# Layer two of an attention and feed-forward kernel: the output product of the third pair of token blocks by seven block products

## The chip, the core and the metric

The kernel is one program on one core of a Trainium2 chip. Its time is the device time of one execution in microseconds (us); of a kernel that ran several times the median is given. TensorE is called PE below, VectorE DVE, ScalarE ACT, GpSimd POOL, and SyncE, which issues the DMAs, SP.

## What is computed

Causal attention with a decay, and then two feed-forward layers on 2304 tokens of 512 values. The change lies in the second layer, `_moe2_ref`:

```python
def reference(**kwargs):
    ...
    attn_out = _attn_ref(**attn_kwargs)
    x = attn_out.transpose(0, 2, 1, 3).reshape(B * S, H * D)   # 2304 x 512
    x = _moe_ref(x=x, **moe_kwargs)
    return _moe2_ref(x=x, **moe2_kwargs)

def _moe2_ref(x, w_in, w_out, alpha):        # w_in 512 x 2048, w_out 2048 x 512
    h = x @ w_in
    g = np.maximum(h, 0.0) + alpha * np.minimum(h, 0.0)
    return (g @ w_out).astype(np.float32)
```

## The kernel before

**Tiling.** The 2304 tokens are three pairs of token blocks, a block being 384 tokens (`NB`); a pair p has its results in the tile `R[p]`. The 2048 middle features are eight groups g of 256, and a group is two feature blocks of 128. One step of the program is a *set* (layer, g, p). In layer two the sets with p = 0 and 1 come first, for all groups; then the sets with p = 2, in the group order 6, 7, 0, 1, 2, 3, 4, 5, close the program.

**A set's input product** is `x @ w_in` on its pair and group, a product of 2 by 2 blocks. It is already made with seven block products instead of eight (`product`, named 1, 5, 6, 3, 7, 2, 4 in their order), each of six matmuls of 384 columns: two slices of the contraction by three terms. A number is kept as a rounded high part and a low rest, and the terms are high by high, high by low and low by high. PSUM sums are completed by ACT copies (`keep`) and DVE additions (`add`). `activate` then makes g of one token block n and feature block i: `first` (ACT, Relu), `second` (DVE), `third` (ACT casts the high part, POOL subtracts it for the low part).

**A set's output product** is `g @ w_out`. It is made as six pieces (`piece`), one for every 128 tokens, each of six matmuls of 512 columns: two feature blocks by three terms. Here g is the stationary operand. DVE adds each piece from its PSUM bank (three of them, `ps_o`) to `R[p]` (`flush`); in the first group of a pair ACT copies instead, and in the last group a DMA writes the rows out.

**Order.** All engines work in the order in which the program was written. A set's seven products are interleaved with the pieces of the set before it, as a string says: `SEQ[1] = "1q5q6q3q7q2q4"`, where q is a piece and every character is one step. `later(d, ...)` puts work behind the step d characters on, `aside(d, ...)` the same, after `later`'s. After the last set six pieces run alone (the *drain*).

**Side work.** During the sets with p = 0 the float64 weights of the next group are converted: tables as `CONV_EVEN` name operations (`ho0`, `lo0` and so on) and the steps at which they run. Converted weights are kept in DRAM, and the sets with p = 2 load them again (`load_w`: 1792 KB of `wi` and 1024 KB of `wo`).

Of the kernel before, what the change touches and what calls it, by code (L numbers as in the profile page):

```python
# [8 lines left out]
F32 = mybir.dt.float32  # L9
# [12 lines left out]
def decay_attention_ffn2_kernel(ctx, tc, qk, v, f, wi1, wo1, wi2, wo2, alpha, out):  # L22
# [59 lines left out]
    wi_d = [[dram.tile([128, 2, 7 * KH * 128], F32, name=f"wid{ff}{g}") for g in range(NG)] for ff in range(2)]  # L82
    wo_d = [[dram.tile([128, 2, FT * DM], F32, name=f"wod{ff}{g}") for g in range(NG)] for ff in range(2)]

    f_d = [dram.tile([128, 4, KH * 256], F32, name=f"fd{g}") for g in range(NC)]
# [36 lines left out]
    def conv_ops(ff, g, cache=False, held=(), tags="abdbc"):  # L122
# [46 lines left out]
        def combine(name):  # L169
            d, a, b, op = SUM[name]  # L170
            nc.gpsimd.tensor_tensor(out=blk(*d), in0=blk(*a), in1=blk(*b), op=op)

        PART = {"a": (0, 2, 0, 0), "b": (2, 4, 1, 0), "c": (4, 6, "S", 0), "d": (6, 7, 1, 0), "o0": 0, "o1": 1}

# [34 lines left out]
        for name in SUM:  # L209
            ops[name] = lambda name=name: combine(name)  # L210
        for name in PART:
            ops["h" + name] = lambda name=name: high(name)
            ops["l" + name] = lambda name=name: low(name)
# [66 lines left out]
    def attention():  # L280
        with ExitStack() as ax:
# [399 lines left out]
    for ff in range(2):  # L681
        sets += [(ff, g, p) for g in gorder[ff][0] for p in range(NPR - 1)]
        if ff == 0:
            sets[1:3] = [(0, 1, 0), (0, 0, 1)]
        sets += [(ff, g, NPR - 1) for g in gorder[ff][1]]
    slot_of = {(0, 0): 0, (0, 1): 1, (0, 2): 0, (1, 0): 1, (1, 1): 0, (1, 2): 1}

    now, at, behind = [0], {}, {}

    def later(d, fn):  # L690
        at.setdefault(now[0] + d, []).append(fn)
# [4 lines left out]
    def activate(s, gt, i, n, h, d):  # L696
        ff, g, p = s
        if n not in gt:
            gt[n] = {}
        hold = {}  # L700

        def first():
            t = P["tp"].tile([128, NB], F32, tag="t", name="t")
# [16 lines left out]
        def third():  # L720
            gt[n][i] = P["gp"].tile([128, 2, NB], F32R, tag=f"g{n}", name=f"g{n}", bufs=3 - n)
            nc.scalar.copy(out=gt[n][i][:, 0], in_=hold["g"])  # L722
            nc.gpsimd.tensor_sub(out=gt[n][i][:, 1], in0=hold["g"], in1=gt[n][i][:, 0].bitcast(F32))  # L723

        later(d, first)
        later(d + 1, second)
        later(d + 1, third)

# [37 lines left out]
    def piece(s, gt, n, c):  # L766
# [35 lines left out]
        later(0, flush)  # L802

    def side_work(s):

        ff, g, p = s

        def conversion(ops, text, keep, scale=1, shift=0, first=0, last=10 ** 6):
            for name, t in table(text, first, last):
                if keep or name[0] != "w":  # L810
                    aside(t * scale + shift, ops[name])
# [14 lines left out]
        if p == 0 and (1 if ff else 2) <= g + 1 < NG and not (ff == 0 and g < 2):  # L826
            ops, keep = conv_ops(ff, g + 1), g + 1 < NG - 2
            cached = ff == 1 and g + 1 < NC
            for text in ((CONV_TURN if cached else CONV_EVEN,) if ff else (CONV_A, CONV_B)):
                conversion(ops, text, keep, 1, 3 if ff and not cached else 5)  # L830
        if p == NPR - 1:
# [21 lines left out]
    def run():  # L853
        prev = None
        for q, s in enumerate(sets + [None]):
            pieces = []
            if prev is not None:
                ps, pgt = prev
                pieces = [lambda n=n, c=c: piece(ps, pgt, n, c)
                          for n in (1, 0) for c in range(KD if ps[0] == 0 else NB // 128)]  # L860
            c, gt = {}, {}
            if s is None:
                seq = "q" * len(pieces)
            else:
                seq = FIRST[q] if q < len(FIRST) else SEQ[ps[0]]
            if s is not None and q != 1:
# [83 lines left out]
```

## Time and profile before

| what | value |
|---|---|
| median of three runs | 960.58 us (960.13 to 962.03) |
| the profiled execution | 962.06 us, its span 960.3 us, granted TensorE clock 0.998 |
| busy in the span | PE 950.0 us, DVE 695.9, POOL 593.6, ACT 535.2 |
| layer two, p = 2, before the drain | eight sets, 822.1 to 948.23 us, 15.77 us each |
| drain | 948.23 to 957.35 us, then the last DMA |

The busy time of PE counts matmuls that overlap, so that 99% does not mean that no matmul waited. The times that matter here are distances between starts.

### The profile page before, as it was taken

How to read it: one execution, taken by the hardware profiler on the slowest of the kernel's cores; microseconds unless marked ns; L12 is line 12 of the kernel's file. 1: busy time of each engine (PE TensorE's matmuls, PEld its weight loads, DVE VectorE, ACT ScalarE, POOL GpSimd, SP SyncE). 2: the span in 40 equal slices, each digit the busy share in tenths (PEclk: the TensorE clock that was granted, in tenths of full speed). 3: DMA queues.
4: the chain of work that ended last, by engine and by line, in shares of the span. 5: the costliest groups of instructions: out<-in, count | busy, mean ns of one | idle time of the engine just before them, and what ended most of it. 6: DMA issues, size and time to landing. Idle time of an engine off the chain costs nothing.

```text
span 960.3 us, 15782 instructions
## 1 busy us (share of the span) xinstructions
PE 950.0 (99%) x5525; PEld 860.1 (90%) x5525; DVE 695.9 (72%) x1227; ACT 535.2 (56%) x1316; POOL 593.6 (62%) x586
## 2 busy tenths in 40 slices
PE   8999999999999999999999999999999999999998
PEld 5777777798999999999999999989899898999897
DVE  7899998858687877786788565267789777535454
ACT  5888887856654555554644365645444545443231
POOL 7678998666666466585765299546655659423131
PEclk9999999999999999999999999999999999999999
DMA  6666777301444244111677623414534410344441
GB/s 217 220 192 205 221 243 212 110 23 44 160 181 160 104 187 187 66 44 34 223 294 292 255 77 125 161 56 165 186 116 159 174 58 34 113 184 164 198 165 66
DMA packets 36195, 145.79 MB, mean 152 GB/s; under 512 B 4860, under 2 KB 4860, under 8 KB 33012
## 3 DMA queue, kind: packets, MB, share of 16 engines
q1 hardware_dynamic: 36112, 144.79, 42.6%
q8 instruction: 43, 0.70, 0.3%
q14 instruction: 36, 0.29, 0.1%
q10 hardware_dynamic: 4, 0.00, 0.0%
HBM read 97.21 MB, written 43.42 MB: 146 GB/s over the span
## 4 chain that ended last, share of the span: by engine, by line
PE 92%; DVE 4%; POOL 1%; issue 1%; ACT 1%; DMA 1%; ACTq 0%; DVEq 0%; SPq 0%; POOLq 0%
PE o L780 21%; PE hA L740 20%; PE o L778 20%; PE hC L740 10%; PE hB L740 5%; PE tp L420 4%; PE pv L478 4%; PE sc L389 2%; PE sc L390 2%; PE sc L401 1%; PE sc L403 1%; PE sc L391 1%; PE tr L458 1%; POOL xl L250 1%; PE pv L510 0%
## 5 line engine op out<-in xcount | busy, mean ns | idle before, releaser
L723 POOL TENSOR_TENSOR g<-t,g 128x384 fp32r<-128x384 f32 x192 | 205.6, 1072 | 284.0 <-ACT g L722 267.5
L778 PE MATMUL o<-g,wo 128*128 128x384 f32 x1152 | 230.8, 339 | 1.2 <-POOL g L723 1.1
L740 PE MATMUL hA<-xh,wi 128*128 128x384 f32 x768 | 224.2, 337 | 0.6 <-ACT p L372 0.3
L780 PE MATMUL o<-wo,g 128*128 128x512 f32 x864 | 223.2, 394 | 0.0
L778 PEld LDWEIGHTS o<-g,wo 128*128 128x128 f32 x1152 | 204.1, 188 | 2.4 <-POOL g L723 2.0
L722 ACT CAST g<-t 128x384 fp32r<-128x384 f32 x192 | 98.7, 514 | 176.6 <-DVE t L717 91.9
L780 PEld LDWEIGHTS o<-wo,g 128*128 128x128 f32 x864 | 160.6, 188 | 25.7
L798 DVE TENSOR_TENSOR r<-o,r 128x512 f32<-128x512 f32 x126 | 86.7, 688 | 86.1 <-PE o L780 85.7
L740 PEld LDWEIGHTS hA<-xh,wi 128*128 128x128 f32 x768 | 141.5, 188 | 4.1 <-DVE hD L754 0.6
L740 PE MATMUL hA<-xl,wi 128*128 128x384 f32 x384 | 129.6, 337 | 0.0
L787 DVE SCALAR_TENSOR_TENSOR r<-o,r 128x384 f32<-128x384 f32 x168 | 92.3, 553 | 46.8 <-PE o L778 45.9
L740 PE MATMUL hC<-xh,wi 128*128 128x384 f32 x384 | 114.1, 338 | 0.0
L372 ACT ACTIVATE p<-sc,nm 128x128 f32<-128x128 f32 (+2 forms) x144 | 80.3, 561 | 20.2 <-DVE nm L365 16.6
L365 DVE TENSOR_REDUCE nm<-sc 128x1 f32<-128x128 f32 (+2 forms) x144 | 71.5, 507 | 13.2 <-PE sc L391 8.2
L740 PEld LDWEIGHTS hA<-xl,wi 128*128 128x128 f32 x384 | 72.1, 188 | 3.2
L740 PEld LDWEIGHTS hC<-xh,wi 128*128 128x128 f32 x384 | 70.9, 188 | 2.1 <-issue 0.2
L250 POOL TENSOR_TENSOR xl<-r,xh 128x384 fp32r<-128x384 f32 x59 | 68.5, 1173 | 2.1 <-ACT xh L245 1.6
L420 PE MATMUL tp<-ident,p 128*128 128x128 f32 x384 | 66.7, 276 | 0.3 <-ACT pt L435 0.3
L745 ACT COPY s<-hA 128x384 f32<-128x384 f32 x96 | 45.8, 477 | 36.1 <-PE hA L740 35.8
L740 PE MATMUL hC<-xl,wi 128*128 128x384 f32 x192 | 64.8, 337 | 0.0
L740 PE MATMUL hB<-xh,wi 128*128 128x384 f32 x192 | 57.1, 338 | 0.0
L754 DVE TENSOR_TENSOR hC<-hC,s 128x384 f32<-128x384 f32 x48 | 27.1, 564 | 40.7 <-PE hC L740 38.9
(150 smaller groups left out, 1744.5 us busy)
## 6 DMA issues: line engine op xcount, KB each, us to landing
wid<-wi SPq DMA_DIRECT2D x24, 896.0 KB
wi<-wid SPq DMA_DIRECT2D x12, 1792.0 KB
rqk<-in_qk SPq DMA_DIRECT2D x32, 608.0 KB
raw<-in_wi SPq DMA_DIRECT2D x32, 512.0 KB
raw<-in_wo SPq DMA_DIRECT2D x32, 512.0 KB
wod<-wo SPq DMA_DIRECT2D x24, 512.0 KB
wo<-wod SPq DMA_DIRECT2D x12, 1024.0 KB
vt<-in_v SPq DMA_DIRECT2D x16, 320.0 KB
```

Of the source, the lines that this page charges most:

```text
L250: e.tensor_sub(out=XS[k][1][:, b, c], in0=x, in1=XS[k][0][:, b, c].bitcast(F32))
L365: last = waits("V", nc.vector.tensor_reduce(out=nm, in_=src, axis=AX.X if n == 1 else AX.XY, op=ALU.max, negate=True), last)
L372: last = waits("A", nc.scalar.activation(out=o, in_=src, func=AF.Exp, bias=nm, scale=1.0, accum_out=dst), last)
L420: nc.tensor.transpose(tp[:, j, :], pt[:, 128 * j:128 * j + 128], ident)
L722: nc.scalar.copy(out=gt[n][i][:, 0], in_=hold["g"])
L723: nc.gpsimd.tensor_sub(out=gt[n][i][:, 1], in0=hold["g"], in1=gt[n][i][:, 0].bitcast(F32))
L740: nc.tensor.matmul(out=h, lhsT=a, rhs=b[:, x, kc], start=new and kc + e == 0, stop=kc == KH - 1 and e == 2, skip_group_check=not new)
L745: nc.scalar.copy(out=c[k], in_=h)
L778: nc.tensor.matmul(out=o[:, 0:NB], lhsT=a[:, cs], rhs=b, start=st, stop=sp)
L780: nc.tensor.matmul(out=o, lhsT=b[:, cs], rhs=a, start=st, stop=sp)
L787: later(0, lambda: nc.vector.scalar_tensor_tensor(out=acc, in0=o[:, 0:NB], scalar=1.0 / 6.0, in1=acc, op0=ALU.mult, op1=ALU.add))
L798: nc.vector.tensor_add(out=acc, in0=o, in1=acc)
```

## The change

For the first seven of the eight groups of pair 2 in layer two (the list `seven`) the output product too is made with seven block products of the 2 by 2 blocks of g (two token blocks by two feature blocks) and of `w_out` (two feature blocks by two halves of 256 columns). The eighth group stays as it was. A block product is three chunks of 128 tokens by three terms: nine matmuls of 256 columns, so 63 of 256 columns for a set in place of 36 of 512. They stand in eleven pieces (`PLAN7`): "4" is two chunks of product 4, "45" the third chunks of 4 and 5 in one bank, "7-" the third chunk of 7 alone. The products are summed over the seven groups in places of their own (`kept`: the four quarters of `R[2]`, two raw tiles, one `wb` tile) and combined in the last of the sets (`sum7`). Sums of blocks of g are made by POOL (`sums`), and each of the seven left operands has its own ACT cast and POOL subtraction. Differences of weight blocks are made in the conversion (`t1` to `t4` on POOL; `v1` to `v4` on DVE for groups 7 and 0), written to DRAM (`wt_d`), loaded as 512 KB for a set and split by two casts on ACT and two subtractions on DVE (`weights7`).

```diff
+    SEQ7 = "1q5qq6qq3qq7qq2q4q"
+    PLAN7 = ("4", "5", "45", "1", "6", "16", "7", "7-", "2", "3", "23")
+    LAST7 = "v1 54 v3 54 v2 55 u0 55 v4 55 u1 56"
+    WT7 = {5: 0, 7: 1, 4: 2, 6: 3}
...
+        def differ(name):
+            b11, b12, b21, b22 = (f32(2 + t)[:, k] for t in range(2) for k in range(2))
+            d, a, b = {"1": (b11, b12, b11), "3": (b12, b22, b12), "2": (b22, b22, b11), "4": (b21, b22, b21)}[name[1]]
+            (nc.vector if name[0] == "v" else nc.gpsimd).tensor_sub(out=d, in0=a, in1=b)
...
-    CONV_EVEN = "... ho1 28 lo1 29 wi0 40 wi1 43 wo0 46 wo1 48"
+    CONV_EVEN = "... ho1 28 lo1 29 t1 29 t3 29 t2 30 u0 30 t4 30 u1 31 wi0 40 wi1 43 wo0 46 wo1 48"
...
+        def sums():
+            a11, a12, a21, a22 = (gt.get(("f", x, y)) for x in range(2) for y in range(2))
+            if (n, i) == (1, 1):
+                gt["f", 5] = temp("wc")[:, 0:NB]
+                nc.gpsimd.tensor_add(out=gt["f", 5], in0=a22, in1=a21)
+            elif (n, i) == (0, 0):
+                gt["f", 6], gt["f", 7] = temp("wd")[:, 0:NB], a21
+                nc.gpsimd.tensor_sub(out=gt["f", 6], in0=gt["f", 5], in1=a11)
+                nc.gpsimd.tensor_sub(out=a21, in0=a11, in1=a21)
+            else:
+                gt["f", 3] = temp("wc")[:, 0:NB]
+                nc.gpsimd.tensor_sub(out=gt["f", 3], in0=a12, in1=gt["f", 6])
...
+        if s in seven:
+            k = {(1, 1): 4, (0, 0): 1, (0, 1): 2}.get((n, i))
+            if k:
+                more = {4: (5,), 1: (6, 7), 2: (3,)}[k]
+                gap = len(more)
+                later(d + 2, lambda: high7(k, hold["g"]))
+                later(d + 2, sums)
+                later(d + 3, lambda: low7(k, hold["g"]))
+                for x in more:
+                    later(d + 3 + gap, lambda x=x: high7(x, gt["f", x]))
+                    later(d + 4 + gap, lambda x=x: low7(x, gt["f", x]))
+            return
...
+    def piece7(s, gt, text):
...
+        for slot, (k, c) in enumerate(work):
...
+            for e, (x, y) in enumerate(((a[:, 0], b[0]), (a[:, 0], b[1]), (a[:, 1], b[0]))):
+                nc.tensor.matmul(out=o[:, hd * slot:hd * slot + hd], lhsT=x[:, cs], rhs=y,
+                                 start=slot == 0 and e == 0, stop=e == 2, skip_group_check=slot > 0)
...
+        def flush():
+            if j == 0 and len(text) == 1:
+                nc.scalar.copy(out=dst, in_=src)
+            elif j == 0:
+                nc.vector.tensor_copy(out=dst, in_=src)
+            else:
+                nc.vector.tensor_add(out=dst, in0=src, in1=dst)
...
+        if text == "16":
+            sum7(1, nc.gpsimd, 6, 1, 6, ALU.add)
+        if text == "7-":
+            sum7(1, nc.gpsimd, 7, 6, 7, ALU.add)
+            sum7(3, nc.gpsimd, 6, 6, 5, ALU.add)
+            sum7(4, nc.vector, 4, 7, 4, ALU.subtract)
+            sum7(5, nc.vector, 5, 7, 5, ALU.add)
+        if text == "23":
+            sum7(2, nc.vector, 2, 1, 2, ALU.add)
+            sum7(3, nc.vector, 3, 6, 3, ALU.add)
...
+        fetch7()
+        for h in range(2):
+            aside(8 + 2 * h, lambda h=h: high7(h))
+            aside(9 + 2 * h, lambda h=h: low7(h))
```

The first place is POOL in a set with p = 2 in the middle of the stretch. Before, a set gives it four low parts (`g1` is token block 1, `g0` token block 0); the rows are those of one set and the first two of the next.

```order
L723 TENSOR_TENSOR g1_10252<-t_10242,g1_10252 128x384
L723 TENSOR_TENSOR g1_10275<-t_10264,g1_10275 128x384
L723 TENSOR_TENSOR g0_10296<-t_10286,g0_10296 128x384
L723 TENSOR_TENSOR g0_10315<-t_10299,g0_10315 128x384
L723 TENSOR_TENSOR g1_10383<-t_10373,g1_10383 128x384
L723 TENSOR_TENSOR g1_10406<-t_10395,g1_10406 128x384
```

After it, one set gives POOL these eleven (L766, L769, L770 and L773 are `sums`, L760 the low parts; in their order the low parts belong to products 4, 5, 1, 2, 6, 7, 3).

```order
L766 TENSOR_TENSOR wc_10309<-t_10288,t_10261 128x384
L760 TENSOR_TENSOR g1_10307<-t_10288,g1_10307 128x384
L760 TENSOR_TENSOR g1_10329<-wc_10309,g1_10329 128x384
L769 TENSOR_TENSOR wd_10344<-wc_10309,t_10320 128x384
L770 TENSOR_TENSOR t_10261<-t_10320,t_10261 128x384
L760 TENSOR_TENSOR g0_10342<-t_10320,g0_10342 128x384
L773 TENSOR_TENSOR wc_10365<-wa_10332,wd_10344 128x384
L760 TENSOR_TENSOR xh0_81<-wa_10332,xh0_81 128x384
L760 TENSOR_TENSOR g0_10385<-wd_10344,g0_10385 128x384
L760 TENSOR_TENSOR g0_10387<-t_10261,g0_10387 128x384
L760 TENSOR_TENSOR xh0_81<-wc_10365,xh0_81 128x384
```

What moved: four operations became eleven of the same size, and the low part of product 6 (`g0_10385<-wd_10344`) is the ninth of them.

The second place is DVE at the end of the last set and the beginning of the drain. Before (L754 is `add`, L717 `second`, L798 `flush`):

```order
L754 TENSOR_TENSOR hB_10789<-hB_10789,s_10703 128x384
L798 TENSOR_TENSOR r2_85<-o_10801,r2_85 128x512
L717 SCALAR_TENSOR_TENSOR t_10808<-t_10808,alpha_sb_76,hB_10789 128x384
L717 SCALAR_TENSOR_TENSOR t_10821<-t_10821,alpha_sb_76,hA_10696 128x384
L798 TENSOR_TENSOR r2_85<-o_10823,r2_85 128x512
```

After (L816 is `add`, L740 `second`, L922 the `flush` of `piece7`, L930 `sum7`, L860 the `flush` of the drain's pieces; `raw_9986` holds product 7's sum, which POOL adds to):

```order
L816 TENSOR_TENSOR hB_11238<-hB_11238,s_11106 128x384
L922 TENSOR_TENSOR r2_85<-o_11246,r2_85 128x2x256
L930 TENSOR_TENSOR r2_85<-raw_9986,r2_85 128x2x256
L930 TENSOR_TENSOR r2_85<-raw_9986,r2_85 128x256
L740 SCALAR_TENSOR_TENSOR t_11255<-t_11255,alpha_sb_76,hB_11238 128x384
L930 TENSOR_TENSOR r2_85<-raw_9986,r2_85 128x2x256
L930 TENSOR_TENSOR r2_85<-raw_9986,r2_85 128x256
L740 SCALAR_TENSOR_TENSOR t_11270<-t_11270,alpha_sb_76,hA_11099 128x384
L922 TENSOR_TENSOR r2_85<-o_11272,r2_85 128x512
L860 TENSOR_TENSOR r2_85<-o_11286,r2_85 128x512
```

What moved: four combining additions that read POOL's sum now stand ahead of the two last `second` and of the flush that frees the bank of piece "23".

## Rows read from the trace of the kernel before

**Rows 1.** Page, part 1: busy us, share of the span, instructions.
```profile
PE 950.0 (99%) x5525; PEld 860.1 (90%) x5525; DVE 695.9 (72%) x1227; ACT 535.2 (56%) x1316; POOL 593.6 (62%) x586
```
**Rows 2.** Windows, one set each: us, busy by engine (count), PEclk, DMA share, GB/s.
```profile
759.03:774.80 15.77, 15.77 (x80) 14.22 (x79) 15.23 (x25) 7.50 (x16) 6.79 (x7) 1.00 0.28 99
...
885.17:900.93 15.76, 15.76 (x80) 14.20 (x79) 7.86 (x14) 5.24 (x11) 4.07 (x4) 1.00 0.49 186
```
**Rows 3.** Timeline, PE, a set with p = 2: start, duration, engine, line, tiles, count.
```profile
838.77 1.56 PE L780 MATMUL o<-wo,g 128*128 128x512 f32 x6
840.17 0.34 PE L740 MATMUL hC<-xh,wi 128*128 128x384 f32 x1
...
841.22 1.56 PE L780 MATMUL o<-wo,g 128*128 128x512 f32 x6
```
**Rows 4.** Timeline, last set: from product 7 to the low part it leads to.
```profile
942.98 0.34 PE L740 MATMUL hA<-xh,wi 128*128 128x384 f32 x1
...
943.16 1.56 PE L780 MATMUL o<-wo,g 128*128 128x512 f32 x6
943.43 0.56 DVE L754 TENSOR_TENSOR hD<-hA,s 128x384 f32<-128x384 f32 x1
944.09 0.49 ACT L708 ACTIVATE t<-hD 128x384 f32<-128x384 f32 x1
...
944.76 0.69 DVE L798 TENSOR_TENSOR r<-o,r 128x512 f32<-128x512 f32 x1 [0.77 <-PE o L780]
...
945.37 0.61 DVE L717 SCALAR_TENSOR_TENSOR t<-t,alpha_sb,hD 128x384 f32<-128x384 f32 x1
...
945.89 0.56 DVE L754 TENSOR_TENSOR hB<-hB,s 128x384 f32<-128x384 f32 x1
946.06 0.51 ACT L722 CAST g<-t 128x384 fp32r<-128x384 f32 x1 [1.48 <-DVE t L717]
...
946.65 1.02 POOL L723 TENSOR_TENSOR g<-t,g 128x384 fp32r<-128x384 f32 x1 [1.44 <-ACT g L722]
```
**Rows 5.** Timeline, PE in the attention: matmuls of 288 and of 256 columns.
```profile
57.05 0.30 PE L401 MATMUL sc<-k,q 128*128 128x288 f32 x1
57.19 0.29 PE L403 MATMUL sc<-k,q 68*128 68x288 f32 x1
...
64.92 0.28 PE L390 MATMUL sc<-k,q 68*128 68x256 f32 x1
65.04 0.23 PE L391 MATMUL sc<-maskb,identb 128*128 128x128 bf16 x1
```
**Rows 6.** Timeline, POOL, operations of 128x384 one behind the other.
```profile
808.45 1.01 POOL L242 TENSOR_TENSOR r<-r 128x384 f32<-128x384 f32 x1
809.43 1.02 POOL L723 TENSOR_TENSOR g<-t,g 128x384 fp32r<-128x384 f32 x1
810.41 1.37 POOL L242 TENSOR_TENSOR r<-r 128x384 f32<-128x384 f32 x1
811.74 1.02 POOL L723 TENSOR_TENSOR g<-t,g 128x384 fp32r<-128x384 f32 x1
```
**Rows 7.** Timeline, DVE, beside the second and third of these.
```profile
809.27 0.69 DVE L798 TENSOR_TENSOR r<-o,r 128x512 f32<-128x512 f32 x1
810.35 0.56 DVE L250 TENSOR_TENSOR xl<-r,xh 128x384 fp32r<-128x384 f32 x1 [0.40 <-ACT xh L245]
```
**Rows 8.** Timeline, layer one: PE and its weight load waiting for a POOL low part.
```profile
221.17 2.07 POOL L723 TENSOR_TENSOR g<-t,g 128x384 fp32r<-128x384 f32 x2
...
222.22 1.15 PE L778 MATMUL o<-g,wo 128*128 128x384 f32 x5 [0.65 <-POOL g L723]
```
**Rows 9.** Groups by form, POOL, whole span: busy us, mean ns, idle before.
```profile
L189 POOL TENSOR_TENSOR wi<-wa,wi 128x512 fp32r<-128x512 f32 x16 | 21.0, 1311 | 0.3 <-ACT wi L185 0.3
...
L171 POOL TENSOR_TENSOR wa<-wa 128x256 f32<-128x256 f32 x15 | 11.1, 738 | 0.6
```
**Rows 10.** Timeline, the drain: PE, and DVE's first and last flush of its pieces.
```profile
948.76 7.86 PE L780 MATMUL o<-wo,g 128*128 128x512 f32 x33
...
951.06 0.69 DVE L798 TENSOR_TENSOR r<-o,r 128x512 f32<-128x512 f32 x1 [0.46 <-PE o L780]
...
956.66 0.69 DVE L798 TENSOR_TENSOR r<-o,r 128x512 f32<-128x512 f32 x1 [0.71 <-PE o L780]
```

More of the change, by code (lines that the diff above doesn't have):

```diff
@@ L210, in conv_ops @@
             ops[name] = lambda name=name: combine(name)
+        for name in ("t1", "t2", "t3", "t4", "v1", "v2", "v3", "v4"):
+            ops[name] = lambda name=name: differ(name)
+        for t in range(2):
+            ops[f"u{t}"] = lambda t=t: differ_out(t)
         for name in PART:
@@ L685, in decay_attention_ffn2_kernel @@
         sets += [(ff, g, NPR - 1) for g in gorder[ff][1]]
+    seven = [(1, g, NPR - 1) for g in gorder[1][1][:-1]]
     slot_of = {(0, 0): 0, (0, 1): 1, (0, 2): 0, (1, 0): 1, (1, 1): 0, (1, 2): 1}
@@ L697, in activate @@
         ff, g, p = s
-        if n not in gt:
+        if n not in gt and s not in seven:
             gt[n] = {}
@@ new lines, in weights7, with fetch7, high7, low7 @@
+    def weights7(s):
+        ff, g, p = s
+        tw = tees(gorder[ff][1].index(g))
+        def fetch7():
+            nc.sync.dma_start(out=tw[:, 1].bitcast(F32), in_=wt_d[g])
+        def high7(h):
+            nc.scalar.copy(out=tw[:, 0, 2 * h:2 * h + 2], in_=tw[:, 1, 2 * h:2 * h + 2].bitcast(F32))
+        def low7(h):
+            nc.vector.tensor_sub(out=tw[:, 1, 2 * h:2 * h + 2], in0=tw[:, 1, 2 * h:2 * h + 2].bitcast(F32),
+                                 in1=tw[:, 0, 2 * h:2 * h + 2].bitcast(F32))
+        if s == seven[0]:
+            ops = conv_ops(1, 0, tags="cdabc")
+            for t, names in ((0, "p2 p3"), (4, "v1 v3"), (5, "v2 u0"), (6, "v4 u1")):
+                for name in names.split():
+                    aside(t, ops[name])
+        fetch7()
+        for h in range(2):
+            aside(8 + 2 * h, lambda h=h: high7(h))
+            aside(9 + 2 * h, lambda h=h: low7(h))
@@ L804, in side_work, with conversion @@
     def side_work(s):
         ff, g, p = s
-        def conversion(ops, text, keep, scale=1, shift=0, first=0, last=10 ** 6):
+        def conversion(ops, text, keep, scale=1, shift=0, first=0, last=10 ** 6, second=None):
             for name, t in table(text, first, last):
+                if name[0] in "tu" and ((1, second, NPR - 1) not in seven or second == NG - 1):
+                    continue
                 if keep or name[0] != "w":
@@ L826, in side_work @@
         if p == 0 and (1 if ff else 2) <= g + 1 < NG and not (ff == 0 and g < 2):
-            ops, keep = conv_ops(ff, g + 1), g + 1 < NG - 2
+            ops, keep = conv_ops(ff, g + 1, tags="abdcc" if ff else "abdbc"), g + 1 < NG - 2
             cached = ff == 1 and g + 1 < NC
             for text in ((CONV_TURN if cached else CONV_EVEN,) if ff else (CONV_A, CONV_B)):
-                conversion(ops, text, keep, 1, 3 if ff and not cached else 5)
+                conversion(ops, text, keep, 1, 3 if ff and not cached else 5, second=g + 1 if ff else None)
+            if ff and g + 1 == NG - 1:
+                for name, t in table(LAST7):
+                    aside(t, ops[name])
+        if s in seven:
+            weights7(s)
         if p == NPR - 1:
@@ L860, in run @@
                           for n in (1, 0) for c in range(KD if ps[0] == 0 else NB // 128)]
+                if ps in seven:
+                    pieces = [lambda text=text: piece7(ps, pgt, text) for text in PLAN7]
             c, gt = {}, {}
```

76 lines of the change are left out of this document (71 added, 5 removed).

## The prediction

> **What bounds the kernel now.** I read the page's busy times first [rows 1]: PE is covered for 99% of the span, the other engines for at most 72%. Windows of single sets come next [rows 2]: a set with p = 2 in the middle of the stretch lasts 15.77 us, PE without a hole, DVE busy 7.86, ACT 5.24, POOL 4.07, the DMA engines half used. That PE has no hole says little, since its busy time overlaps, so I read distances between starts [rows 3]: from a piece to the next product 1.40 us (six matmuls of 512 columns, 0.233 each), from a product to the next piece 1.05 us (six of 384, 0.175 each). Seven products and six pieces make 15.75: PE works at its pace and waits for nobody. What must stay ahead of it is the way from a product to the low part that a piece reads [rows 4]: product 7 ends at 943.16, its sum starts at 943.43, the low part at 946.65, 3.5 us later. POOL then has much room.
>
> **What the change saves on PE.** A matmul of 256 columns: two of 288 start 0.14 or 0.13 apart with a weight load each, and one of 256 leaves 0.12 to the next [rows 5]. Scaled from 512 columns it is 0.117, scaled from the longer run of 288s 0.119; I take 0.119, with 0.134 as the upper bound if the weight load and not the columns set the 288s. A set's output product then costs 63 x 0.119 = 7.50 against 36 x 0.233 = 8.39, the set 14.87 against 15.77. Seven such sets (the pieces of the seven groups run in the set behind each, 837.9 to 948.2 us) would give back 6.2 us. With 0.134 they would give nothing. The Trainium skill, "TensorE: Matmul & The Clock Gate", Back-to-back issue gap, gives N / 2.4 + 2.5 ns, so 109 ns for 256 columns; for 384 it gives 162 where the rows have 175, so the rows decide. By it the sum below would come out some 1 us lower.
>
> **What it adds to the others, for a set.** DVE: eleven flushes for six (ten of 0.69, one shorter) and two subtractions; back to back a flush takes 0.61, an `add` about 0.47 and a `second` 0.52, as their starts show [rows 4]. That is 10 x 0.61 + 0.33 + 2 x 0.61 + 3 x 0.47 + 4 x 0.52 = 11.1 us of 14.9: it fits. ACT: five more casts, three of 0.51 [rows 4] and two that I bound by a flush's 0.69: 5.24 + 1.53 + 1.38 = 8.2 us: fits. DMA: 512 KB beside 2816, so a share of 0.58 for 0.49, asked for at the set's start and read eight steps later: hidden. POOL: eleven operations for four. Back to back they start 0.98 apart [rows 6], 10.8 us of 14.9. It fits as a sum, but not as a chain.
>
> **The chain that goes round.** The low part of product 6 is POOL's ninth operation of a set, and piece "6" stands at the eighth place of the next set's eighteen; behind it in PE's order stands product 7, which starts POOL's next round. I follow one round, 0 being the end of that low part. PE: about 0.05 until PE goes on and 0.11 for the weight load that it then has to see through ([rows 8]: the first of the two low parts ends about 222.17, PE starts at 222.22, and its first five starts span 0.82, which is 1.15 less the last's 0.33, instead of 4 x 0.175), four matmuls left of "6" (0.48), so 0.64; product 3 to 1.69; "16" and "7" to 3.12; product 7 to 4.17. DVE in its order: `add` for 3 at 1.96 (0.27 after its product, [rows 4]), flush "16" 2.6, a weight half 3.2, `second` for 3 at 3.8, flush "7" 4.3, `add` for 7 at 4.9 (it could have begun at 4.44), a weight half 5.4, flush "7-" 6.0, `second` for 7 at 6.35, done 6.95. POOL starts the sum for 5 at 7.03. Nine operations: eight distances of 0.98, a wait of 0.13 for the cast of 5, the last operation 1.02: 8.97. The round takes 16.0 us, where PE has work for 14.9 and the set before took 15.77. So PE stands about 1.1 us at piece "6" in every set, and the saving turns into a loss of 0.2.
>
> **The sum.** In the first of the seven sets the low part of 6 lands late too: in the set ahead product 7 ends at 10.85, POOL begins 3.5 later [rows 4], its nine operations with a wait of 0.45 for `second` of 2 end at 23.7, that is 7.9 into the next set. There ACT takes seven of the flushes, DVE's queue is shorter and the first round about 15.6; then five rounds of 16.0; behind the last, PE has 8.75 left (0.64, three more pairs of product and pieces, "23"). 7.9 + 15.6 + 80.0 + 8.75 = 112.25 against 7 x 15.77 = 110.4: +1.85.
>
> **The end.** In the last set POOL combines sums between its low parts: the low part of 3 ends at 12.6, product 6's sum (1.31 and 0.74, [rows 9], a little less back to back) at 14.55, the low part of 7 at 15.5, product 7's sum at 17.5. DVE is done with flush "3" at 15.0 and, in order, waits 2.5 us for that sum. Behind it stand two `second` and the flush of "23", which ends at 21.3 instead of about 18. The drain's third piece needs that bank and would start at 18.7 (before, the drain ran without a gap, six flushes 1.40 apart, [rows 10]): PE waits 2.7. The bounds: 2.0 if DVE goes on after the first half of the sum, 3.3 if POOL's next sum and DVE's, both with two inputs in SBUF, stretch each other as below.
>
> **Elsewhere.** The differences for groups 1 to 4 and 6 are 20 POOL operations of 0.74 [rows 9] in sets with p = 0 where POOL is busy 6.8 us but DVE 15.2 of 15.8 [rows 2]. A POOL operation beside a DVE one with two SBUF inputs took 1.37 instead of 1.02, beside a flush from PSUM 1.02 [rows 6, 7]. So DVE may be pushed back there; nothing as long as it has the 1 us that low parts are ahead, up to 1 us a set otherwise; I take 0.1 for each of five. The eight differences on DVE in the set at 822 us find it half idle: nothing, 0.5 at most. The fourteen stores and two loads of differences on SP's queue stand ahead of fetches with steps of room: nothing. Together: 1.85 + 2.7 + 0.5 = +5.0.
>
> **Its own time.** Span 960.3 gives 965.3; the profiled execution's 962.06 gives 967.1. The median of the runs was 960.58, so I predict 965.6. (About 0.2%, 1.9 us, is what can be told from no change.)
>
> **Rivals.**
> *POOL is not last: faster.* If the nine operations took under 7.8 us (0.87 each), or the way from product 7 to POOL were 1.1 shorter, every low part would be in time, sets would take 14.9, and 6.2 us come back: 954.4, or 957.1 with the end's stall. For it: POOL's share is only 73%. Against it: not one of the operations in a row starts under 0.97 behind another [rows 6], and 3.5 us is the calm value of the way. Chance 0.11.
> *It comes out even.* A round of 15.75 (0.25 less: DVE's queue ahead of `second` shorter by half an operation) makes the seven sets equal, and with the end at 2 or less the time lies between 958.7 and 962.5. Chance 0.16.
> *POOL and DVE stretch each other: slower still.* With two of the nine operations at 1.37 [rows 6, 7] a round is 0.7 longer, six rounds 4.2 us: 969.8. For it: DVE now has two subtractions with both inputs in SBUF in each set. Against it: by the walk they fall between 3.2 and 6.0, where POOL has just run dry. The Trainium skill, "GPSIMD Engine Reference", Specifications, names this contention for DVE instructions with two SBUF inputs; the rows agree. Chance 0.13.
> *The forecast*, 962.5 to 968.5: chance 0.60. The matmul at 0.134 lies in it: sixteen of them in a round, 0.24 each round, +1.4.
>
> **The numbers.** 965.6 is the forecast's. The range 961.2 to 970.2 leaves out the first rival and half of the second. Faster by over 0.2%: 0.11; within: 0.16; slower: 0.73.
>
> **What would show it.** Right: sets of 16.0 us from the third on; PE waiting about 1 us in each at piece "6", ended by POOL; POOL in trains of eleven, 0.98 apart, with a pause of 4 to 5 us; DVE waiting 2 to 3 us for POOL at the end, and the drain 11 us long instead of 8.4. Wrong: sets of 14.9; no wait for POOL; matmuls of 256 columns at 0.134; POOL operations at over 1.1 beside DVE; gaps on PE before 820 us.

## The result, and the profile after

| kernel | runs | median (lowest to highest) | ratio to before, 95% interval |
|---|---|---|---|
| before | 6 | 961.28 us (960.13 to 962.24) | |
| after | 6 | 968.58 us (967.23 to 969.33) | 1.0075, 1.0062 to 1.0088 |

The change makes the kernel 7.3 us slower, where 5.0 were forecast; the time lies within the forecast's range of 961.2 to 970.2 us, 3.0 us above its 965.6. (The forecast counted from 960.58, the median of three runs of before; with six it is 961.28.) The profiled execution of after took 969.33 us, its span 967.5 us, 7.2 more than before's. Where these 7.2 us lie is read from the start of product 2 in each set:

| stretch, us | before | after | difference |
|---|---|---|---|
| start of the program to product 2 of the set ahead of the seven (834.20, 833.31) | 834.20 | 833.31 | -0.9 |
| from there to product 2 of the last set, seven distances | 110.36 | 112.28 | +1.9 |
| from there to the span's end | 15.7 | 21.9 | +6.2 |

The first line is no effect of the change: the 0.9 us are there already at the first product 2 of layer one (194.17 and 193.27 us), ahead of everything that the change touches, and the ten executions below lie between 191.9 and 194.3 us at that point. One reason is the granted clock: in before's execution it fell at 10.7 to 14.1 us, in the start-up that all kernels share, and in this one of after it did not; five of the ten others have that dip. All sets of layer two ahead of the seven have the same distances in both, 15.74 to 15.78 us in the last eight.

First the page's busy times of after (part 1), beside [rows 1]:

```profile
PE 948.3 (98%) x5714; PEld 866.5 (90%) x5714; DVE 733.1 (76%) x1291; ACT 550.3 (57%) x1352; POOL 665.4 (69%) x661
```

PE has 189 more instructions and is busy 1.7 us less; POOL has 75 more and 71.8 us more. The windows of after, from product 2 to product 2, are the ones to set beside the second of [rows 2] (columns as there: us, busy of PE, PEld, DVE, ACT and POOL, granted clock, DMA share, GB/s):

```profile
833.31:850.64 17.33, 15.45 (x101) 14.67 (x100) 9.20 (x15) 10.22 (x23) 10.77 (x11) 1.00 0.44 168
850.64:866.06 15.42, 15.09 (x108) 14.89 (x107) 10.19 (x18) 8.18 (x18) 10.78 (x11) 1.00 0.57 221
913.79:929.68 15.89, 15.10 (x107) 14.90 (x106) 11.84 (x21) 7.31 (x16) 10.78 (x11) 1.00 0.57 217
...
945.60:967.50 21.90, 14.95 (x62) 12.00 (x60) 13.73 (x22) 2.71 (x6) 9.76 (x10) 0.84 0.19 72
```

A set costs 15.9 us although PE is busy for only 15.1 of them; the first costs 17.3, and in the last stretch the clock was not always fully granted. What PE waits for in a set of 15.9 is in the timeline of PE and POOL (start, duration, engine, line, tiles, count, idle time before and what ended it; L766, L769, L770, L773 are `sums`, L760 the low parts, L906 the pieces):

```profile
931.54 1.02 POOL L766 TENSOR_TENSOR wc<-t 128x384 f32<-128x384 f32 x1 [5.12 <-DVE t L740]
...
939.22 0.40 PE L906 MATMUL o<-xl,g 128*128 128x256 f32 x2
939.39 1.00 POOL L760 TENSOR_TENSOR g<-wd,g 128x384 fp32r<-128x384 f32 x1
...
940.34 1.02 POOL L760 TENSOR_TENSOR g<-t,g 128x384 fp32r<-128x384 f32 x1
940.44 0.74 PE L906 MATMUL o<-xl,g 128*128 128x256 f32 x4 [0.82 <-POOL g L760]
...
941.31 1.02 POOL L760 TENSOR_TENSOR xh<-wc,xh 128x384 fp32r<-128x384 f32 x1
```

POOL works off eleven operations from 931.54 to 942.33 without a pause. The ninth, at 939.39, is the low part of 6 (`g<-wd`); it ends at 940.39, and PE, which has done the first two matmuls of piece "6", goes on at 940.44. It stood 0.95 to 0.98 us there in each set from the third of the seven on.

The end, all engines:

```profile
947.59 0.68 DVE L922 TENSOR_TENSOR r<-o,r 128x512 f32<-128x512 f32 x1
...
948.70 1.29 POOL L930 TENSOR_TENSOR raw<-raw 128x512 f32<-128x512 f32 x1
...
949.16 2.94 PE L842 MATMUL o<-wo,g 128*128 128x512 f32 x12
949.95 0.73 POOL L930 TENSOR_TENSOR raw<-wb,raw 128x256 f32<-128x256 f32 x1
950.03 2.63 DVE L930 TENSOR_TENSOR r<-raw,r 128x512 f32<-128x512 f32 x2 [1.76 <-POOL raw L930]
950.64 1.73 POOL L930 TENSOR_TENSOR raw<-raw,r 128x512 f32<-128x512 f32 x1
952.34 0.90 POOL L930 TENSOR_TENSOR wb<-wb,r 128x256 f32<-128x256 f32 x1
952.58 0.60 DVE L740 SCALAR_TENSOR_TENSOR t<-t,alpha_sb,hB 128x384 f32<-128x384 f32 x1
953.11 1.02 DVE L930 TENSOR_TENSOR r<-raw,r 128x512 f32<-128x512 f32 x2
...
954.20 0.61 DVE L740 SCALAR_TENSOR_TENSOR t<-t,alpha_sb,hA 128x384 f32<-128x384 f32 x1
954.74 0.68 DVE L922 TENSOR_TENSOR r<-o,r 128x512 f32<-128x512 f32 x1
...
955.47 8.46 PE L842 MATMUL o<-wo,g 128*128 128x512 f32 x24 [3.38 <-DVE r L922]
```

DVE is idle behind the flush at 947.59 until POOL has the first half of its product-7 sum (948.70 to 949.99). The first pair of combining operations then takes 2.63 us, and POOL's next sum beside it 1.73 and 0.90 where its last one took 1.29 and 0.73. The flush of "23", at 954.74, is behind all that, and PE needs its bank: two of the drain's six pieces are done by 952.1, the third starts at 955.47, where [rows 10] have a drain without a gap. Then 24 matmuls take 8.46 us. The windows say why (columns as above):

```profile
952.00:954.00 2.00, 0.09 (x1) 0.00 (x0) 2.00 (x4) 0.73 (x2) 1.38 (x3) 1.00 0.00 0
954.00:956.00 2.00, 0.53 (x1) 0.50 (x2) 1.92 (x5) 0.68 (x2) 1.54 (x2) 0.60 0.00 0
956.00:958.00 2.00, 2.00 (x6) 1.55 (x5) 2.00 (x5) 0.00 (x0) 0.44 (x1) 0.50 0.35 131
...
962.00:964.00 2.00, 1.93 (x9) 1.23 (x7) 0.72 (x2) 0.00 (x0) 0.00 (x0) 1.00 0.35 131
```

Behind the stretch in which PE stood, the granted clock is 0.50, the lower level (1.2 GHz of 2.4). The matmuls of 512 columns start 0.43 us apart there, and 0.23 at 1.00.

### The profile page after: what moved, and what is told of

The parts are those of the page before. It is cut to its first block, busy times and chain, and to the rows that moved or that the text cites. A ratio compares the mean times of both kernels' runs of the same rounds, so it can differ in the third digit from the quotient of the medians.

```text
span 967.5 us, 16523 instructions
## 1 busy us (share of the span) xinstructions
PE 948.3 (98%) x5714; PEld 866.5 (90%) x5714; DVE 733.1 (76%) x1291; ACT 550.3 (57%) x1352; POOL 665.4 (69%) x661
## 4 chain that ended last, share of the span: by engine, by line
PE 83%; DVE 7%; POOL 5%; issue 3%; ACT 2%; DMA 1%; DVEq 0%; POOLq 0%; ACTq 0%; SPq 0%
PE o L840 19%; PE hA L802 18%; PE o L842 15%; PE hC L802 9%; PE hB L802 4%; PE pv L492 4%; PE tp L434 4%; PE sc L403 2%; PE sc L404 2%; PE o L906 2%; POOL g L760 1%; PE sc L415 1%; PE sc L417 1%; PE sc L405 1%; PE tr L472 1%
## 5 line engine op out<-in xcount | busy, mean ns | idle before, releaser
L746 POOL TENSOR_TENSOR g<-t,g 128x384 fp32r<-128x384 f32 x164 | 177.5, 1083 | 173.9 <-ACT g L745 167.2
L745 ACT CAST g<-t 128x384 fp32r<-128x384 f32 x164 | 84.3, 514 | 149.4 <-DVE t L737 74.7
L842 PE MATMUL o<-wo,g 128*128 128x512 f32 x612 | 160.7, 399 | 3.4 <-DVE r L922 3.4
L842 PEld LDWEIGHTS o<-wo,g 128*128 128x128 f32 x612 | 115.6, 191 | 22.7 <-DVE r L922 3.8
L860 DVE TENSOR_TENSOR r<-o,r 128x512 f32<-128x512 f32 x90 | 61.7, 686 | 43.2 <-PE o L842 42.9
L816 DVE TENSOR_TENSOR hC<-hC,s 128x384 f32<-128x384 f32 x48 | 27.0, 563 | 37.1 <-PE hC L802 31.5
```

What stands on the lines that cost most here:

```text
L842: nc.tensor.matmul(out=o, lhsT=b[:, cs], rhs=a, start=st, stop=sp)
L860: nc.vector.tensor_add(out=acc, in0=o, in1=acc)
```

## The experiments

Two causes were to be tested: the **round** (the ninth place of the needed low part in POOL's row) for the seven sets, and **DVE waiting in order for POOL's combining**, with the clock behind it, for the end. The rivals were that POOL or DVE are simply full, and that the seven-product set is dear in itself. All ratios are to before's runs on the same chip. A *round* below is a set in the middle of the stretch, from the third of the seven on.

### Combining a set earlier: e1_six

```diff
-    seven = [(1, g, NPR - 1) for g in gorder[1][1][:-1]]
+    seven = [(1, g, NPR - 1) for g in gorder[1][1][:-2]]
```

> The changed kernel with six of the eight groups by seven block products instead of seven, so that the sums are combined in the set before the last, and the drain has nothing of them. The theory (DVE waits for POOL's sum, holds a PSUM bank for 3.9 us, and PE's clock falls to half behind that wait, 2.5 us): the drain is as in the kernel before, without a wait over 0.3 us and at full clock; rounds of 15.9 us stay; the last set 15.8 to 16.7 since the late second halves may hold it up; about 4.5 us less than the changed kernel, 963.5 to 964.5. Rival (the clock falls at the end for another reason, such as how long the program has run): the drain's matmuls still start 0.43 apart, and the time is about 966.5. Rival (the loss lies in the rounds alone): 968 or more.

965.03 us (964.07 to 966.11), ratio 1.0039 (1.0024 to 1.0054). The rounds stayed at 15.91 to 15.93 us and the end was before's, 15.83 us. But the plain set into which the combining moved took 17.68 us. Its timeline around the wait:

```profile
935.24 2.64 DVE L930 TENSOR_TENSOR r<-raw,r 128x512 f32<-128x512 f32 x2 [1.77 <-POOL raw L930]
...
938.50 0.51 ACT L745 CAST g<-t 128x384 fp32r<-128x384 f32 x1 [5.03 <-DVE t L740]
...
940.50 0.47 ACT L807 COPY s<-hA 128x384 f32<-128x384 f32 x1
...
941.03 0.44 PE L802 MATMUL hA<-xh,wi 128*128 128x384 f32 x1 [1.66 <-ACT s L807]
```

It is the same stand-still of DVE (1.77 us idle, the pair at 2.64); this time ACT is held up by it, and PE's next product waits for a PSUM bank that ACT empties. So 6.2 us at the end became 0.1 there and 1.9 a set earlier, more than was expected of that set, and the time lies 0.5 us above what was expected.

### POOL's row against the pieces: e2_plan, e5_plan_late7

The first puts piece "2" ahead of "6", "16", "7" and "7-", so that the low part of 6 is needed later:

```diff
-    PLAN7 = ("4", "5", "45", "1", "6", "16", "7", "7-", "2", "3", "23")
+    PLAN7 = ("4", "5", "45", "1", "2", "6", "16", "7", "7-", "3", "23")
```

> The changed kernel with the eleven pieces in another order and nothing else: 4, 5, 45, 1, 2, 6, 16, 7, 7-, 3, 23. The theory (the round from POOL's ninth operation over piece 6 and product 7 back to POOL): piece 6 now stands two places later, only 2.4 us ahead of product 7's end instead of 4.2, so that round takes 14.2 and no longer binds; the round over the low part of 2, the eighth operation, takes 15.0 to 15.2. Rounds of 14.9 to 15.2 instead of 15.91, about 5 us less in the sets; at the end DVE's wait stays but hits less, 0 to 2 us less: 962 to 964. Rival (POOL's eleven operations bind as a sum, or DVE's queue does): rounds stay at 15.9 and the time within 1 us of 968.6.

962.03 us (960.52 to 964.32, ten runs), ratio 1.0009 (0.9999 to 1.0018). The rounds fell from 15.91 us to between 15.15 and 15.22, and the end from 21.9 to 19.3. One of them (columns as above):

```profile
895.77:910.99 15.22, 15.12 (x108) 14.91 (x107) 11.87 (x21) 7.30 (x16) 10.77 (x11) 1.00 0.60 225
```

That was expected: one line, no operation fewer on any engine, and the rounds give back 0.7 each.

The second has that order too, and makes POOL's sum for operand 7 three steps later, where the low part of 7 needs it:

```diff
-                nc.gpsimd.tensor_sub(out=a21, in0=a11, in1=a21)
...
                 for x in more:
-                    later(d + 3 + gap, lambda x=x: high7(x, gt["f", x]))
-                    later(d + 4 + gap, lambda x=x: low7(x, gt["f", x]))
+                    e = d + (2 if x == 7 else 0)
+                    if x == 7:
+                        later(e + 2 + gap, lambda: nc.gpsimd.tensor_sub(out=gt["f", 7], in0=hold["g"], in1=gt["f", 7]))
+                    later(e + 3 + gap, lambda x=x: high7(x, gt["f", x]))
+                    later(e + 4 + gap, lambda x=x: low7(x, gt["f", x]))
```

> The new order of pieces of e2_plan, and besides it POOL's sum of operand 7 (second, not first, half of a pair that it makes two steps after product 2) is made three steps later, just ahead of the low part that needs it, so that the low part of 2 stands two operations earlier in POOL's row. POOL has as many operations as before. Theory (each round is set by where the needed low part stands in POOL's row, not by how many operations POOL has): the 0.25 us that e2_plan still waited at piece 2 goes, rounds of 14.87 to 14.95 us in place of 15.2, and the wait in the second seven-product set shrinks by 0.8: 959.0 to 960.5 us, from 962.0 for e2_plan. Rival (POOL or DVE is full and the rounds stay at 15.1 to 15.2, with a wait at another piece): 961.5 to 962.5.

960.53 us (959.95 to 962.87, ten runs), ratio 0.9997 (0.9987 to 1.0006). That is no different from before, and at the upper edge of what was expected. The rounds are 14.82 to 14.95 us with no wait of PE in them: all the change's saving on PE, with POOL's eleven operations as in after. One of them:

```profile
909.09:923.95 14.86, 14.86 (x107) 14.86 (x107) 11.53 (x21) 7.30 (x16) 10.77 (x11) 1.00 0.61 232
```

The first of the seven took 16.16 instead of 17.3. The end was not the 19.3 of e2_plan but 20.1 (PE stood 2.6 and 1.3 us). At this pace of PE the number of POOL's operations is no limit; their order was.

### The sums on DVE: e3_dve_sums

```diff
-                nc.gpsimd.tensor_add(out=gt["f", 5], in0=a22, in1=a21)
+                nc.vector.tensor_add(out=gt["f", 5], in0=a22, in1=a21)
...
```

and the same for the other three.

> The changed kernel with the four sums of a set made by DVE instead of POOL. The theory (nine POOL operations between product 7 and the low part of 6): six of the nine remain... of these the sums leave five low parts and some DVE time, the round falls to 13 or 14 and PE binds at 14.9: sets 14.9 to 15.2, about 7 us less there; the end's loss stays at about 6 us: 960.5 to 962.5. Rival (DVE is the narrow place: 11.1 us of 14.9 and 2 more, now with two SBUF inputs beside POOL, 1.37 for 1.02): rounds of 15.9 or over, 968 or more.

965.36 us (964.27 to 967.01), ratio 1.0040 (1.0027 to 1.0053): neither expected time came, though the rounds were the rival's. The first two sets took 15.31 and 14.84 us, the others 16.05 to 16.14, PE waiting 1.1 to 1.2 us in each for a DVE flush. In its timeline:

```profile
900.43 1.23 DVE L769 TENSOR_TENSOR wd<-wc,t 128x384 f32<-128x384 f32 x1
...
901.21 1.33 POOL L760 TENSOR_TENSOR g<-t,g 128x384 fp32r<-128x384 f32 x1
901.58 1.37 DVE L770 TENSOR_TENSOR t<-t 128x384 f32<-128x384 f32 x1
...
904.13 0.98 PE L906 MATMUL o<-xl,g 128*128 128x256 f32 x6 [1.01 <-DVE r L922]
```

Two of the sums take 1.23 and 1.37 us beside POOL's low parts, which take 1.33 instead of 1.02; the other two, with POOL idle, 0.54 and 0.55 (898.13 and 904.00). Where the sums lie beside POOL the work is not taken off the path; it is stretched on both.

### The weight halves earlier: e4_halves_early

```diff
-            aside(8 + 2 * h, lambda h=h: high7(h))
-            aside(9 + 2 * h, lambda h=h: low7(h))
+            aside(3 + 2 * h, lambda h=h: high7(h))
+            aside(4 + 2 * h, lambda h=h: low7(h))
```

> The changed kernel with the casts and subtractions of the weight differences five steps earlier in a set (steps 3 to 6 instead of 8 to 11), out of DVE's queue between piece 6 and the second for product 7. The theory that the round includes DVE's queue: two times 0.61 us leave it, of which 0.4 to 0.7 count, rounds of 15.2 to 15.5, 2.5 to 4 us less: 964.5 to 966. If they now meet POOL's low parts (two SBUF inputs), POOL loses up to 0.35 twice a round and the gain goes: 968 to 969. Rival (POOL's sum of operations alone binds): rounds stay at 15.9.

965.96 us (964.46 to 967.07), ratio 1.0048 (1.0033 to 1.0063). The rounds went to 15.67 to 15.75 us, 0.2 less, not the 0.4 to 0.7 expected. That the time still lies in the expected range is due to the first of the seven sets, which fell from 17.3 to 16.1 us. In the rounds the halves now lie beside POOL's last operations:

```profile
904.50 1.37 DVE L955 TENSOR_TENSOR xl<-xl 128x512 fp32r<-128x512 f32 x1 [1.02 <-ACT xl L952]
905.25 1.49 POOL L760 TENSOR_TENSOR g<-t,g 128x384 fp32r<-128x384 f32 x1
...
906.39 0.90 DVE L955 TENSOR_TENSOR xl<-xl 128x512 fp32r<-128x512 f32 x1
906.71 1.46 POOL L760 TENSOR_TENSOR xh<-wc,xh 128x384 fp32r<-128x384 f32 x1
...
907.82 0.55 DVE L816 TENSOR_TENSOR hC<-hC,s 128x384 f32<-128x384 f32 x1
```

In the rounds of after these halves lie where POOL is idle, and take 0.68 us. Here they take 1.37 and 0.90, and a flush waits behind them, so that the `add` for product 3 (the last line) starts 0.8 us behind the end of that product (907.00), in after 0.25 (926.41 behind 926.16). What the halves no longer take from DVE's queue behind that `add` they take ahead of it. POOL's sum then follows the end of the low part of 6 by 6.87 us, in after by 7.06.

### The end: e10_no_combine, e8_warm, e6_tail

First its whole price, by leaving the combining out:

```diff
-        if s != seven[-1]:
+        if True:
             return
```

> The changed kernel without the seven combining sums of the end (twice each): the output of the third pair lacks them, so this is only a measure of what they cost. Theory: all of the 6.2 us by which the end is longer than before is theirs (PE standing for VectorE behind POOL, and the clock behind that): the last stretch is 15.7 to 15.9 us as before, the clock does not fall, 962.0 to 962.9 us, with the 1.9 us of the rounds left over before's time. Rival (part of it is the seven-product set before the end itself, its flushes or pieces): the last stretch 17 to 20 us, 963.5 to 966.

963.40 us (962.41 to 963.97, nine runs), ratio 1.0023 (1.0013 to 1.0033). The time is 0.5 us above what was expected and just short of the rival's, but the last stretch is the theory's: 15.7 us, with no stand-still of PE in it, and the clock falls only at 959.9 us, behind the last matmul (957.6), as it does in before:

```profile
945.92:961.60 15.68, 12.09 (x62) 10.16 (x60) 8.19 (x14) 2.71 (x6) 3.29 (x4) 0.95 0.26 100
```

So all 6.2 us are the combining's. What is left over before's time, 2.2 us by the ratio, is the seven sets (+2.1 in its profiled execution).

Then the clock, with the wait left as it is: 18 matmuls that nothing reads, where PE stood.

```diff
                 if ch == "q":
+                    if s is None and len(pieces) == 4:
+                        w, x = P["ps_h"].tile([128, 512], F32, tag="C", name="hC", bufs=1), XS[1][0]
+                        for _ in range(18):
+                            nc.tensor.matmul(out=w[:, 0:NB], lhsT=x[:, 0, 0, 0:128], rhs=x[:, 0, 0], start=True, stop=True)
                     pieces.pop(0)()
```

> The changed kernel with 18 matmuls of 128x384 that nothing reads, put on PE where it stood for 3.4 us in the end (ahead of the third block product of the last set; 18 x 0.175 = 3.15 us, into an unused PSUM bank). The wait itself stays. Theory (2.5 us of the end are the clock that fell to 1.2 GHz behind the stand, 13 matmuls at 0.427 in place of 0.232): the clock stays at 1.0 and the kernel takes 965.8 to 966.5 us. Rival (the clock falls whatever PE does there, or the flushes are what the end waits for): 968.3 to 969 us.

967.30 us (966.64 to 967.80), ratio 1.0064 (1.0049 to 1.0079): 0.8 us above what was expected, and below the rival. PE in the end, and one window:

```profile
951.81 3.31 PE L1049 MATMUL hC<-xh 128*128 128x384 f32 x18
955.37 5.85 PE L842 MATMUL o<-wo,g 128*128 128x512 f32 x24 [0.25 <-DVE r L922]
```

```profile
956.00:958.00 2.00, 2.00 (x10) 1.64 (x9) 2.00 (x4) 0.00 (x0) 0.35 (x1) 1.00 0.34 131
```

The third piece starts at 955.37, as it did in after (955.47), since the bank comes no sooner. But the same 24 matmuls take 5.85 us instead of 8.46, at a granted clock of 1.00. That is the clock's part of the end: 2.6 us in these two executions, and the stand-still's the other 3.6. Between the medians only 1.3 us lie. The mean granted clock of every run is on record: 0.996 in four of after's six and 0.998 in two, 1.000 in two of e8_warm's four and 0.998 in the others. The dip in the start-up alone gives 0.998 (before's profiled execution), the fall in after's end 0.996. So in at least four of after's runs the clock lost more than that dip; for the other two it stays open where it fell.

Last, an attempt to take the stand-still away by making POOL's last sum and DVE's first combining later, behind the flush of "23":

```diff
-            sum7(3, nc.gpsimd, 6, 6, 5, ALU.add)
-            sum7(4, nc.vector, 4, 7, 4, ALU.subtract)
-            sum7(5, nc.vector, 5, 7, 5, ALU.add)
+            sum7(6, nc.gpsimd, 6, 6, 5, ALU.add)
+            sum7(6, nc.vector, 4, 7, 4, ALU.subtract)
+            sum7(6, nc.vector, 5, 7, 5, ALU.add)
```

> The changed kernel with one thing moved: in the last set, the POOL sum of products 6 and 5 and the two pairs of combining operations of VectorE that need POOL's sum 7 are made 2 to 3 steps later, behind the flush of piece 23 and behind the last two Leaky steps. Theory of the end (PE stood for 3.9 us because VectorE waited in order for POOL with the flush of piece 23 queued behind it; the clock fell to 1.2 GHz behind that): the wait and the fall both go, the rounds stay at 15.9; 6.2 us more than before at the end becomes 0.5 to 1.5: 963.0 to 964.5 us. Rival (the combining only moves, and the last rows of the output leave as late): 966 to 968.6 us, with the waits now in front of the last flushes.

968.57 us (966.85 to 970.49), ratio 1.0078 (1.0062 to 1.0095): no gain, the rival was right. In the profiled execution:

```profile
953.04 1.44 POOL L930 TENSOR_TENSOR raw<-raw,r 128x512 f32<-128x512 f32 x1
954.45 0.72 POOL L930 TENSOR_TENSOR wb<-wb,r 128x256 f32<-128x256 f32 x1
954.52 1.53 DVE L930 TENSOR_TENSOR r<-raw,r 128x512 f32<-128x512 f32 x2 [1.15 <-POOL raw L930]
955.98 0.68 DVE L860 TENSOR_TENSOR r<-o,r 128x512 f32<-128x512 f32 x1
...
956.80 4.64 PE L842 MATMUL o<-wo,g 128*128 128x512 f32 x18 [3.33 <-DVE r L860]
```

The flush of "23" comes at 950.43 now, and PE gets one more piece done. But the drain's own first flush (L860) writes the rows that the combining fills, so it has to stand behind DVE's, and that behind POOL's last sum, which now ends at 955.17. PE stood 3.5 us all the same, one piece later. In this execution, the fastest of the kernel, the clock did not fall (in the slowest run, 970.49 us, its mean was 0.994); so of the four profiles with a stand-still of 3.5 to 3.6 us three show the fall behind it (after, e3_dve_sums, e4_halves_early), and one doesn't.

### Both together, and a version that beats both kernels: e7_best, e9_six_best

The first is e5_plan_late7 with the later combining:

```diff
-            sum7(3, nc.gpsimd, 6, 6, 5, ALU.add)
-            sum7(4, nc.vector, 4, 7, 4, ALU.subtract)
+            sum7(5, nc.gpsimd, 6, 6, 5, ALU.add)
+            sum7(5, nc.vector, 4, 7, 4, ALU.subtract)
             sum7(5, nc.vector, 5, 7, 5, ALU.add)
```

> e5_plan_late7 and the later combining of e6_tail together. If the two causes (the order in POOL's row, and VectorE's wait for POOL ahead of a flush) are separate, the gains add: rounds of 14.87 to 14.95 as in e5_plan_late7, and an end that is 1 to 3.3 us shorter than that of e2_plan (which stood for 1.94 and 1.32 us): 956.5 to 959 us, faster than both kernels. Rival (with PE faster VectorE or POOL is late in the end in another place, the end stays at 19.3 us): 959.5 to 960.5.

963.14 us (961.19 to 963.87, ten runs), ratio 1.0019 (1.0009 to 1.0028): the gains did not add, and it is slower than e5_plan_late7 by 2.6 us. The rounds are those of e5_plan_late7, but PE stood 4.2 us at the fourth of the drain's six pieces, as in e6_tail, and the clock was at 0.5 from 948.9 to 955.7: the end took 22.6 us. The stand-still is hardly longer than the two of e5_plan_late7 together (2.6 and 1.3); what the end is longer by, 2.5 us, is nearly all the clock. The combining found no room in the last set.

So e9_six_best gives it a set: six groups by seven products (the edit of e1_six), order and late sum of e5_plan_late7, and the combining spread behind it.

```diff
-            sum7(3, nc.gpsimd, 6, 6, 5, ALU.add)
-            sum7(4, nc.vector, 4, 7, 4, ALU.subtract)
+            sum7(2, nc.gpsimd, 6, 6, 5, ALU.add)
+            sum7(5, nc.vector, 4, 7, 4, ALU.subtract)
             sum7(5, nc.vector, 5, 7, 5, ALU.add)
...
-            sum7(2, nc.vector, 2, 1, 2, ALU.add)
-            sum7(3, nc.vector, 3, 6, 3, ALU.add)
+            sum7(4, nc.vector, 2, 1, 2, ALU.add)
+            sum7(5, nc.vector, 3, 6, 3, ALU.add)
```

> Six groups of the third pair by seven products in place of seven (as e1_six), with the order of e5_plan_late7, and the combining sums later, spread over the plain set that follows: POOL's sum of 6 and 5 right behind its sum 7, VectorE's combining of 4 and 5 at the start of the next set, of 2 and 3 a step or two behind the first flush of that set. Theory: six rounds at 14.87 to 14.95 save 0.85 each (5.1), the wait in the second seven-product set gives back 0.4, the plain set with the combining is 15.7 to 16.0 because nothing is queued behind a wait of VectorE for POOL, and the end is as before (15.7 to 15.8): 955.8 to 957.5 us, faster than both kernels. Rival (VectorE and POOL, both on SBUF operands, hold each other up in the set with the combining, which takes 17 to 17.7 us as in e1_six): 957.8 to 958.8.

957.75 us (955.74 to 958.24), ratio 0.9964 (0.9952 to 0.9977): faster than before by 3.1 us, than after by some 11 (by the ratios). That is 0.25 us above the expectation and just short of the rival's range. Its windows, a seven-product set, the set with the combining, and the end:

```profile
909.43:924.26 14.83, 14.83 (x108) 14.83 (x106) 11.47 (x21) 6.79 (x15) 10.78 (x12) 1.00 0.48 196
924.26:940.04 15.78, 15.78 (x87) 14.45 (x85) 14.62 (x22) 4.67 (x10) 10.84 (x10) 1.00 0.19 67
940.04:956.20 16.16, 12.33 (x55) 9.74 (x53) 8.72 (x15) 3.44 (x8) 4.08 (x4) 1.00 0.26 99
```

In the set with the combining DVE is busy 14.6 of 15.8 us, four of its operations stretched beside POOL to 5.2 us together, and PE does not wait: nothing that PE needs is queued behind a wait of DVE for POOL. So the rival's 17 to 17.7 us for that set did not come; the end is 0.4 us longer than expected.

## The prediction, point by point

**PE's saving: right.** Twelve matmuls of 256 columns in a row start over 1.42 us, 0.119 each, and a round in which PE waits for nothing takes 14.82 to 14.95 us (e5_plan_late7, e9_six_best), where 14.87 was worked out.

**The round: right.** 16.0 us was walked through, 15.91 came. From the end of the low part of 6 to POOL's next sum it is 7.06 us (923.49 + 0.99 to 931.54; 7.03 in the walk), the nine operations take 8.85 (8.97 in the walk; the terms that it names add up to 8.99, and those of the first set to 23.8 where it has 23.7, too little to matter). PE stands 0.97 instead of 1.1 us, at the piece and behind the operation that were named. e2_plan and e5_plan_late7 show that it is the cause and not only a wait that comes last.

**The seven sets: +1.9 for +1.85**, and that it came so close is luck: two errors cancel. The first round was 0.2 us shorter and the five others 0.1 each, 0.6 in all. The first set was worse by as much: the low part of 6 ended 8.6 us into the next set (7.9 in the walk), since POOL stood 1.2 us for `second` of 2, not 0.45, and PE then 1.6 us at piece "5" as well:

```profile
836.39 1.02 POOL L760 TENSOR_TENSOR g<-t,g 128x384 fp32r<-128x384 f32 x1
836.58 1.38 DVE L955 TENSOR_TENSOR xl<-xl 128x512 fp32r<-128x512 f32 x1
837.87 0.60 DVE L740 SCALAR_TENSOR_TENSOR t<-t,alpha_sb,hB 128x384 f32<-128x384 f32 x1
838.61 1.02 POOL L769 TENSOR_TENSOR wd<-wc,t 128x384 f32<-128x384 f32 x1 [1.20 <-issue]
...
841.60 0.62 PE L906 MATMUL o<-xl,g 128*128 128x256 f32 x3 [1.44 <-POOL g L760]
```

A weight half beside a low part took 1.38 us instead of 0.68, with `second` of 2 queued behind it. This is the third rival's mechanism, in one set only; from the second on the halves fall into POOL's pause, as was said there. e4_halves_early, which moves the halves, has a first set of 16.1 us for 17.3.

**The end: the term that was mis-sized**, 2.7 us for 6.2. POOL's sum was timed well (done at 950.68, 17.5 us into the set that begins at 933.20, for 17.5), and so was PE (the third piece could have begun at 951.93, a matmul's 0.23 us behind the start of the last one, 18.7 for 18.7). What failed is the step from that sum to the flush of "23". DVE went on after the first half of the sum, as the lower bound had it, and then DVE and POOL stretched each other, as the upper bound had it. The pair took 2.63 us, and the flush ended at 955.42 (22.2 us into the set) instead of 21.3. PE stood 3.5 us, more than the upper bound of 3.3. And behind the stand-still the clock fell, for another 2.6 us between the profiled executions of after and e8_warm, a term that the sum did not have at all.

**Elsewhere: +0.5 was not there.** The sets with p = 0, with the differences on POOL, have before's distances to 0.01 us. If DVE was stretched there, it reached PE nowhere.

**The rivals.** *POOL is not last* fell: PE waits for POOL in every set. *It comes out even* is excluded by the interval. *POOL and DVE stretch each other* gave nearly the right time (969.8) for a wrong reason: it put the stretch into six rounds, where there is none; it was in the first set and in the end. The measured 968.58 us lie at the upper edge of *the forecast*'s own 962.5 to 968.5, the side of this rival.

## What to carry to other kernels

Where an engine off the critical path gets a row of operations, its busy share does not tell whether it holds up the others: POOL was busy for 10.8 us in rounds of 15.9 and in rounds of 14.9. Write the row down with the place of the operation that the critical engine needs, and walk one round through all engines; then look for an order in which the needed ones come first, before looking for another engine to do the work. A step at the end of a loop that makes an in-order engine wait for another is dear twice: by what is queued behind the wait, and by the clock of a TensorE that stood. Give it a stretch in which nobody needs what stands behind it, even at the price of leaving one round of the faster scheme out.

## What the runs showed of the hardware

The granted clock fell to 0.5 behind a stand-still of PE of 3.5 us in after (954.4 to 961.2), of 3.6 and 3.5 in e3_dve_sums and e4_halves_early (953.6 to 957.1, 950.6 to 957.5) and of 4.2 in e7_best (948.9 to 955.7); in the profiled executions it did not behind 2.6 us or less (e1_six, e2_plan, e5_plan_late7), nor, in one, behind 3.5 (e6_tail). That is not to say that it never does: three of the ten runs of e5_plan_late7 have a mean clock of 0.996, which no run of before has, and they are its slowest (961.70 to 962.87 us, the other seven 959.95 to 960.74). Where it fell in these three is not shown. Matmuls that nothing reads, put into the stand-still, kept it at 1.0. The price is in the rows, 8.46 us for 24 matmuls that take 5.85 at 1.0. The Trainium skill, "TensorE: Matmul & The Clock Gate", HAM oscillation, says that a TensorE that stands idle between bursts of matmuls has its clock halved; the trace of after agrees (0.50 from 954.4 on), that of e6_tail, with nearly the same stand-still, does not.

POOL and DVE operations with both inputs in SBUF, side by side, stretch to 1.3 to 1.5 us on POOL (1.02 alone) and to 0.9 to 1.4 on DVE (0.68 for a weight half alone). The rows read as turns and not as a slower pace: in after's end POOL's half sum ends at 950.68, and DVE's first combining, begun at 950.03, ends at 951.23; POOL's next, begun at 950.64, ends at 952.37, and DVE's second, begun at 951.16, at 952.66. These three end 0.55, 1.14 and 0.29 us behind the end of the other engine's operation; alone they take 0.68, 1.29 and 0.41. No run tests this further. DVE's flushes, with one input in PSUM, leave POOL's row at 0.97 to 0.98 a step.
